# Early-stage operations moved to other places in their queues in a kernel of memory attention and a SwiGLU feed-forward layer, and two weight scans of the long units moved one beat on

## The chip, the cores and the metric

One core of one Trainium2 chip runs the program. The metric is the device time of one execution in microseconds (us). The time before is 1707.99 us, the median of three runs (1706.39, 1707.99 and 1708.14). A difference of 0.2% is 3.4 us.

## What the kernel computes

The reference takes one sequence `x` of 2048 tokens with 576 channels and makes a mix of two layers, each token with a gate of its own:

```python
g = _sigmoid((x * gate_w).sum(-1, keepdims=True))
a = _A_ref(x, A_wq, A_wk, A_wv, A_wo, A_beta)   # 32 heads of 18, four segments of 512 tokens
b = _B_ref(x, B_w_gate, B_w_up, B_w_down)       # (silu(x @ w_gate) * (x @ w_up)) @ w_down
return g * a + (1 - g) * b
```

`_A_ref` is attention inside a segment, mixed (by a learned `sigmoid(beta)` for each head) with a read of a memory matrix that sums `phi(k) v` over the segments before; `_B_ref` has 4608 hidden channels.

## The kernel before

**Numbers.** The big products work on float32 values that are split in two float16 parts, a high one (the rounded value) and a low one (the rest); a product is three float16 products (high·high, high·low, low·high) in one PSUM bank. Both parts carry a scale, a power of two, and to find it the kernel must first scan the raw weights: ACT squares a block and adds up each row (the helper at L140 for gate and up weights, L1125 in `d_look` for the down weights), PE sums across the partitions (L158), DVE and POOL make the scale of it (L150 to L154, L1137 to L1140).

**Stage 1** (0 to about 229 us) makes Q, K and V of the four segments. A segment has nine chains `n = 0..8` (Q and K) and then eight V steps (L806 on), each followed in segments 1 to 3 by `mem_step`, which reads the memory. Beside the last segment's steps lies what the next stage needs first: the operands of `x` for the first feed-forward units (`first_sum` on POOL, `first_split` with ACT L136 and DVE L137), and the split of the first unit's weights. That split is `w_make`: POOL makes sums of raw blocks (L369), ACT the high part (L373), DVE the low part (L377), SP stores both to a scratch in DRAM (L381, `wc`), for they are wanted again in the second half. `start = w_make(0)` (L799) is a list of such steps with a due number each, in rising order, and the V steps take from its front.

**Stage 2** is the feed-forward layer. It runs over two halves of the tokens and in each over 36 blocks `f` of 128 hidden channels; one (half, f) is a **unit**. Its gate and up products are done by a Strassen-like scheme with seven products, `seven(...)` (PE L1437 and L1440), and behind each product or so stands a `tick()`, eight in a unit. The eight stretches are its **beats**. In the order of one unit: product 0, ACT L1531 copies it; product 1, L1536; product 2, DVE L1540; product 3, ACT L1543; product 4, ACT L1547 and DVE L1548; ACT L1550 makes Silu, product 5, ACT L1552 Silu again; then, in units of the first half with `f % 3 == 0`, L1430 (`exp_table`) reads one number through Exp so that the table for the attention's exponentials is there; two ticks, product 6, DVE L1559 and L1560, the split of the hidden values (ACT L1305, DVE L1308).

Every third unit (`f % 3 == 0`, from f = 3) is a **long unit**. Its beats also hold 16 groups of the down projection for the three blocks before (PE L1171, DVE L1178 for the first three blocks or L1180 later) and steps of the attention (PE L895 and L1011, ACT L1015, POOL L1023 and L1115, DVE L913). PE, ACT and DVE each work through their queue strictly in the order in which the code lists it.

**What sets the order.** Work for a later beat is put in a queue with `defer(k, fn)`, to run `k` beats on. A unit has a plan, a list of `(o, fn)` that is put in with `defer(o + 1, fn)`. In the plan are the next unit's `w_make`; `r_block` (DMA of `rr` at L350, POOL sums L341 to L344, ACT L351, two stores `rc` at L348, DVE L333, a third store), which prepares a remainder of the weights; and `glance(i, k)`, k = 0..7 (L1411 to L1419): the load of a block of 128 x 640 raw weights (DMA L1416, 320 KB) into one of four buffers, and later its squares (ACT L140), which the scale of a coming group of four blocks needs. The offsets of the loads may be negative, then they lie in the unit before the long unit (L1474, `7 + o`). For the down weights, `d_load` (DMA L317, three buffers `draw`) and `d_look` are called from `tick` directly (L1502 to L1508).

**DMA.** All loads and stores are issued by SP (SyncE), one after the other. Where one has to wait (for a buffer, or for a tile to be stored), all behind it wait as well.

Of the kernel before, what the change touches and what calls it, by code (L numbers as in the profile page):

```python
# [36 lines left out]
CH = 3  # L37
# [32 lines left out]
def gated_mix(ctx, tc, xT, xrest, wf, wfr, wfh, wd, wv, wo, beta, cmask, ident, bmask, out):  # L70
# [323 lines left out]
    with ExitStack() as st:  # L394
# [326 lines left out]
        def scan_load(t):  # L721
# [3 lines left out]
            if t in (21, 30):  # L725
# [4 lines left out]
        FSPLIT = {2: [(0, 0)], 3: [(5, 0), (0, 1)], 4: [(1, 0), (4, 0)], 5: [(5, 1), (2, 0)], 6: [(1, 1), (3, 0)],  # L730
                  7: [(3, 1), (4, 1)]}
        for s in range(NSEG):
# [51 lines left out]
            if s == 3:  # L784
# [14 lines left out]
                start = w_make(0)  # L799
            for n in range(8):  # L800
# [23 lines left out]
                else:  # L824
                    if n == 4:
                        wraw_of[1] = [w_load(1, u) for u in range(2)]
                    if n == 0:
                        first_split(2, 1)
                    if n == 1:
                        first_sum(6, 1)  # L830
                    if 2 <= n < 4:
                        first_split(6, n - 2)
                    for k, t, v in ((0, rhs[0][96:], 0.0), (1, kst[0], -1.0), (3, kst[1], -1.0), (4, rhs[1][96:], 0.0)):
# [4 lines left out]
                    if n > 2:  # L838
                        for z in stack_loads(0)[2 * n - 6:2 * n - 4]:
                            nc.sync.dma_start(*z)  # L840
                    for _ in range((0, 1, 2, 2, 2, 2, 2, 2)[n]):
                        if start[0][0] < 8:
                            start.pop(0)[1]()
        flush()
        while start[0][0] < 8:
            start.pop(0)[1]()


    with ExitStack() as st:
# [560 lines left out]
        def glance(i, k):  # L1410
            f, u = 4 * i + k // 2, k % 2  # L1411
            box = []

            def load():
                box.append(x_slot(*next(looks), F32).rearrange("p a b -> p (a b)")[:, :NT * P])
                nc.sync.dma_start(box[0].rearrange("p (k n) -> p k n", n=P), wf[f][:, u])  # L1416

            return [((-2, -1, 0, 1, 3, 4, 4, 5)[k], load),
                    ((2, 2, 3, 4, 5, 6, 6, 7)[k], lambda: square(box[0], 20 + 9 * i + k))]  # L1419

# [22 lines left out]
        for o, fn in start:  # L1443
            defer(o - 7, fn)
        for pos, (half, f) in enumerate(seq):
# [49 lines left out]
            def tick():  # L1495
# [5 lines left out]
                if half == 0:  # L1501
                    g = {(0, 0): f + 2, (2, 2): f + 1, (2, 4): f + 2}.get((q, k), FT) if f > 1 else k if f == 0 and k < CH else FT  # L1502
                    if g < FT:
                        draw[g] = d_load(g)
                    if (f == 1 and 4 <= k < 4 + CH) or (f > 2 and q == 0 and 2 <= k < 2 + CH):
                        d_look(k - 4 if f == 1 else f + k - 2)
                    if (f, k) == (2, 1) or (f > 2 and (q, k) == (0, 5)):
                        d_scale(f // CH)  # L1508
# [175 lines left out]
```

## Time and profile before

| | |
|---|---|
| median of three runs | 1707.99 us |
| the profiled execution itself | 1707.77 us |
| its span | 1705.7 us |
| granted TensorE clock | 1.00 |
| start of the first units of stage 2 (f = 0, 1, 2, 3) | 229.8, 243.9, 253, 267 us |
| starts of the long units f = 6, 9, 12, 15, 18, 21 | 322, 379, 436, 493, 550, 607 us |
| size of a load of `glance`, of `raw`, of `rr` | 320, 256, 128 KB |

The span is what the trace covers, from the first instruction to the last; the execution is 2.1 us longer. A row of the timeline gives the start in us from the start of the span, the duration, engine, line, operation, output and inputs, and in brackets how long the engine had been idle before it and what released it. Rows of PE overlap: a matmul of 512 columns has a row of 0.38 us, and the next one starts 0.22 us after it. So where PE waits, the idle time in brackets is about 0.16 us less than what was lost. Rows of SP are the issue of a DMA; when it lands is seen at the engine that waits for it.

### The profile page before, as it was taken

Reading aid. Unit: us, or ns where it says so; the run is one execution under the profiler, and the core shown is the slowest. Engines: PE = TensorE matmul, PEld = TensorE weight load, DVE = VectorE, ACT = ScalarE, POOL = GpSimd, SP = SyncE. Lnnn points to the kernel's source line nnn. Section 1 sums busy time; section 2 is a strip of 40 time slices with the busy share of each in tenths; the row PEclk is TensorE's granted clock in tenths of the full one; section 3 lists DMA queues with packets and bytes.
Section 4 is the critical chain, followed back from the end, with each engine's and each line's share of the span. In section 5 each row is a group of like instructions: output and inputs, shape, how many; then the busy total and the mean of one; then the engine's idle time right before and its main releaser. Section 6 shows DMA issues by size and latency. Waiting matters only on the chain.

```text
span 1705.7 us, 35389 instructions
## 1 busy us (share of the span) xinstructions
PE 1674.5 (98%) x12269; PEld 1076.9 (63%) x12269; DVE 1300.5 (76%) x3155; ACT 1137.9 (67%) x2064; POOL 879.6 (52%) x1191
## 2 busy tenths in 40 slices
PE   9999999999999999999999999999999999999999
PEld 7898865556655665565556656656656656655587
DVE  7687666789888988898887776777767677665466
ACT  7666566777777777767775776776767676676411
POOL 3336552266656665665453655465546565554121
PEclk9999999999999999999999999999999999999999
DMA  8666776666776675446545386786597588574544
GB/s 288 225 225 226 231 244 213 219 197 182 224 229 208 171 238 193 156 121 197 170 132 178 100 197 161 158 217 157 129 213 179 123 209 182 130 165 123 156 158 146
DMA packets 349542, 314.25 MB, mean 184 GB/s; under 512 B 201268, under 2 KB 266548, under 8 KB 349364
## 3 DMA queue, kind: packets, MB, share of 16 engines
q1 hardware_dynamic: 349364, 312.00, 63.5%
q8 instruction: 96, 1.57, 0.4%
q14 instruction: 82, 0.67, 0.1%
HBM read 186.15 MB, written 99.55 MB: 167 GB/s over the span
## 4 chain that ended last, share of the span: by engine, by line
PE 76%; ACT 7%; DVE 7%; DMA 4%; issue 3%; POOL 1%; SPq 1%; DVEq 0%; ACTq 0%; POOLq 0%
PE bank L1437 30%; PE bank L1171 19%; PE bank L223 10%; PE bank L1440 5%; PE bank L895 3%; PE bank L1011 2%; PE bank L1039 1%; ACT L1550 1%; PE bank L505 1%; DMA raw<-in_wf_dram 1%; PE bank L1041 1%; ACT row L1550 1%; PE bank L973 1%; DVE ya L1180 1%; DVE junk L913 1%
## 5 line engine op out<-in xcount | busy, mean ns | idle before, releaser
L1171 PE MATMUL bank<-dw,hh 128*128 128x320 f16 (+1 forms) x2304 | 435.1, 285 | 9.5 <-DVE ya L1180 6.3
L1171 PE MATMUL bank<-dw,hl 128*128 128x320 f16 (+1 forms) x1152 | 329.0, 286 | 1.2 <-DVE hl L1308 0.6
L1115 POOL TENSOR_TENSOR p<-pe,p 128x512 f16<-128x512 f32 x220 | 272.0, 1237 | 61.7 <-DVE p L1111 34.9
L1171 PEld LDWEIGHTS <-hh 128*128 128x128 f16 x2304 | 224.8, 98 | 95.0 <-issue 15.4
L1015 ACT ACTIVATE pe<-bank 128x512 f32<-128x512 f32 x220 | 130.2, 592 | 161.8 <-PE bank L1011 149.2
L1180 DVE SCALAR_TENSOR_TENSOR ya<-bank,sc,ya 128x320 f32<-128x320 f32 x352 | 177.5, 512 | 76.3 <-PE bank L1171 74.5
L1440 PE MATMUL bank<-xr,rh 128*128 128x512 f16 x504 | 191.0, 379 | 0.0
L913 DVE CUSTOM_DVE_ANT_0 junk<-bank,cm 128x128 bf16<-128x128 f32 (+2 forms) x352 | 169.5, 481 | 20.4 <-PE bank L895 8.7
L1023 POOL TENSOR_SCALAR_AFFINE_SELECT pe<-pe 128x256 f32<-128x256 f32 (+1 forms) x220 | 88.2, 401 | 163.6 <-ACT pe L1015 156.0
L1308 DVE SCALAR_TENSOR_TENSOR hl<-hh,row 128x512 f16<-128x512 f16 x144 | 126.8, 882 | 43.6 <-ACT hh L1305 42.6
L1171 PEld LDWEIGHTS <-hl 128*128 128x128 f16 x1152 | 112.3, 97 | 30.2 <-DVE hl L1308 1.3
L895 PE MATMUL bank<-kst,qst 108*128 108x512 bf16 (+3 forms) x512 | 124.5, 299 | 5.8 <-ACT pe L1015 4.8
L1011 PE MATMUL bank<-qst,kst 111*128 111x512 bf16 (+3 forms) x352 | 103.2, 300 | 1.1 <-DVE acc L984 1.1
L369 POOL TENSOR_TENSOR ws<-raw 128x256 f32<-128x256 f32 x72 | 65.7, 913 | 64.3 <-DMA raw<-in_wf_dram 43.8
L1548 DVE TENSOR_TENSOR row<-bank,row 128x512 f32<-128x512 f32 x72 | 49.7, 690 | 63.8 <-ACT bank L1547 63.7
L223 PE MATMUL bank<-xo,qhi 128*128 128x512 f32 x288 | 92.3, 401 | 0.5 <-DVE xo L133 0.4
L1305 ACT ACTIVATE hh<-row 128x512 f16<-128x512 f32 x144 | 89.1, 619 | 1.8 <-DVE row L1560 1.7
L466 POOL TENSOR_TENSOR q<-qr,q 128x512 bf16<-128x512 f32 x36 | 47.4, 1315 | 82.9 <-ACT q L465 69.7
L1543 ACT ACTIVATE row<-bank 128x512 f32<-128x512 f32 x72 | 42.9, 596 | 68.0 <-PE bank L1440 68.0
L1440 PEld LDWEIGHTS <-rh 128*128 128x128 f16 x504 | 49.3, 98 | 59.5
L1559 DVE SCALAR_TENSOR_TENSOR row<-bank,sc,row 128x512 f32<-128x512 f32 x72 | 53.9, 749 | 43.2 <-PE bank L1440 22.2
L1547 ACT ACTIVATE bank<-bank 128x512 f32<-128x512 f32 x72 | 41.9, 581 | 64.0 <-PE bank L1440 62.0
(1104 smaller groups left out, 4265.0 us busy)
## 6 DMA issues: line engine op xcount, KB each, us to landing
xo<-in_wf_dram SPq DMA_DIRECT2D x65, 320.0 KB
raw<-in_wf_dram SPq DMA_DIRECT2D x72, 256.0 KB
dc<-dw SPq DMA_DIRECT2D x36, 432.0 KB
dw<-dc SPq DMA_DIRECT2D x36, 432.0 KB
rh<-rc SPq DMA_DIRECT2D x72, 168.0 KB
draw<-in_wd_dram SPq DMA_DIRECT2D x36, 288.0 KB
xo<-in_xT_dram SPq DMA_DIRECT2D x33, 256.0 KB
vd<-vps SPq DMA_DIRECT2D x8, 912.0 KB
```

Of the source, the lines that this page charges most:

```text
L223: nc.tensor.matmul(t, st[n], mv[n], start=(n == 0), stop=(n == 13))
L895: nc.tensor.matmul(t[:, c:c + w], qs[:KR, pr, P * i:P * i + P], ks[:KR, pr, 0:w], start=True, stop=True)
L913: nc.vector.tensor_tensor_reduce(junk.bitcast(BF)[:, :w], t[:, c:c + w], cm[:, L - w:L], 1.0, -3.0e38, OP.add, OP.max, m[:, k:k + 1])
L1011: nc.tensor.matmul(t[:, c:c + w], ks[:KR + 3, pr, P * j:P * j + P], qs[:KR + 3, pr, P * j:L], start=True, stop=True)
L1015: nc.scalar.activation(pe, t, AF.Exp, scale=SCALE)
L1115: nc.gpsimd.tensor_sub(p2, pe, p1)
L1171: nc.tensor.matmul(t, p, d[:, q, cs], start=(f == CH * c and n == 0), stop=(f == CH * c + CH - 1 and n == 2))
L1180: nc.vector.scalar_tensor_tensor(ya[:, i, cs], t, inv[c], ya[:, i, cs], op0=OP.mult, op1=OP.add)
L1305: nc.scalar.activation(hi, src, AF.Copy, scale=1.0 / STEP)
L1308: nc.vector.scalar_tensor_tensor(lo, hi, -STEP, src, op0=OP.mult, op1=OP.add)
L1437: nc.tensor.matmul(t, w[:, p, z], x[z][:, q], start=first and n == 0, stop=False, skip_group_check=True)
L1440: nc.tensor.matmul(t, rem[:, RPOS[j]], XR[j], start=False, stop=True, skip_group_check=True)
```

## The change

It moves steps; nothing is computed that was not before, and nothing is left out.

1. In the last segment of stage 1, the split of operand (4, 1) goes from Q/K chain 7 to behind V step 0; (2, 1) from behind V step 0 to 1; the sum (6, 1) from behind V step 1 to 2.
2. Of the first unit's weight split, the steps due at 7 (a store of `wc`, and one high part on ACT) leave the V steps and run in the first beat of the first unit.
3. In unit f = 1 the three `d_look` go from ticks 4 to 6 to ticks 1 to 3; in unit f = 2 `d_scale` from tick 1 to tick 0.
4. In `glance`, the loads of k = 0..3 are issued two beats earlier, and the squares of k = 4 and k = 6 come one beat later. This holds for the seven long units f = 3 to f = 21.

```diff
--- before.py
+++ after.py
@@ -728,7 +728,7 @@
         blocks = {3: [(0, 0)], 4: [(0, 1)], 5: [(0, 2), (1, 0)], 6: [(1, 1)], 7: [(1, 2)]}
         FSUM = {3: [(1, 0), (4, 0)], 4: [(2, 0), (1, 1)], 6: [(4, 1), (2, 1)], 7: [(6, 0)]}
         FSPLIT = {2: [(0, 0)], 3: [(5, 0), (0, 1)], 4: [(1, 0), (4, 0)], 5: [(5, 1), (2, 0)], 6: [(1, 1), (3, 0)],
-                  7: [(3, 1), (4, 1)]}
+                  7: [(3, 1)]}
         for s in range(NSEG):
             upd = upd_gen(s - 1) if s else None
             casts = []
@@ -824,12 +824,10 @@
                 else:
                     if n == 4:
                         wraw_of[1] = [w_load(1, u) for u in range(2)]
-                    if n == 0:
-                        first_split(2, 1)
-                    if n == 1:
+                    if n < 4:
+                        first_split(*((4, 1), (2, 1), (6, 0), (6, 1))[n])
+                    if n == 2:
                         first_sum(6, 1)
-                    if 2 <= n < 4:
-                        first_split(6, n - 2)
                     for k, t, v in ((0, rhs[0][96:], 0.0), (1, kst[0], -1.0), (3, kst[1], -1.0), (4, rhs[1][96:], 0.0)):
                         if n == k:
                             nc.gpsimd.memset(t, v)
@@ -838,11 +836,11 @@
                     if n > 2:
                         for z in stack_loads(0)[2 * n - 6:2 * n - 4]:
                             nc.sync.dma_start(*z)
-                    for _ in range((0, 1, 2, 2, 2, 2, 2, 2)[n]):
-                        if start[0][0] < 8:
+                    for _ in range((0, 1, 2, 2, 2, 2, 0, 0)[n]):
+                        if start[0][0] < 7:
                             start.pop(0)[1]()
         flush()
-        while start[0][0] < 8:
+        while start[0][0] < 7:
             start.pop(0)[1]()
 
 
@@ -1415,8 +1413,8 @@
                 box.append(x_slot(*next(looks), F32).rearrange("p a b -> p (a b)")[:, :NT * P])
                 nc.sync.dma_start(box[0].rearrange("p (k n) -> p k n", n=P), wf[f][:, u])
 
-            return [((-2, -1, 0, 1, 3, 4, 4, 5)[k], load),
-                    ((2, 2, 3, 4, 5, 6, 6, 7)[k], lambda: square(box[0], 20 + 9 * i + k))]
+            return [((-4, -3, -2, -1, 3, 4, 4, 5)[k], load),
+                    ((2, 2, 3, 4, 6, 6, 7, 7)[k], lambda: square(box[0], 20 + 9 * i + k))]
 
         looks = cycle([(6, 0), (6, 1), (5, 0), (5, 1)])
 
@@ -1441,7 +1439,7 @@
 
         draw = {}
         for o, fn in start:
-            defer(o - 7, fn)
+            defer(max(1, o - 7), fn)
         for pos, (half, f) in enumerate(seq):
             if f == 0:
                 yas[half] = yp.tile([P, 8, D], F32, name="ya")
@@ -1502,9 +1500,9 @@
                     g = {(0, 0): f + 2, (2, 2): f + 1, (2, 4): f + 2}.get((q, k), FT) if f > 1 else k if f == 0 and k < CH else FT
                     if g < FT:
                         draw[g] = d_load(g)
-                    if (f == 1 and 4 <= k < 4 + CH) or (f > 2 and q == 0 and 2 <= k < 2 + CH):
-                        d_look(k - 4 if f == 1 else f + k - 2)
-                    if (f, k) == (2, 1) or (f > 2 and (q, k) == (0, 5)):
+                    if (f == 1 and 1 <= k <= CH) or (f > 2 and q == 0 and 2 <= k < 2 + CH):
+                        d_look(k - 1 if f == 1 else f + k - 2)
+                    if (f, k) == (2, 0) or (f > 2 and (q, k) == (0, 5)):
                         d_scale(f // CH)
                     if (f, k) == (2, 7) or (f > 2 and (q, k) == (1, 3)):
                         d_back(f // CH)
```

Behind L830 the changed file's line numbers are two lower than those of before (L1416 becomes L1414, and so on). The numbers behind names are the program's own for a buffer's use and differ between the files.

What SP issues around the border from unit f = 5 to the long unit f = 6; `xo` are the loads of `glance`, `wc` the stores of split weights, `raw`, `draw` and `rr` loads of weights. Before:

```order
L381 DMA wc<-wo__3636 128x512
L312 DMA raw<-in_wf_dram 128x512
L1416 DMA xo_3715<-in_wf_dram 128x640
L381 DMA wc<-wo__3684 128x1024
L1416 DMA xo_3721<-in_wf_dram 128x640
L381 DMA wc<-wo__3699 128x1024
L317 DMA draw<-in_wd_dram 128x576
L350 DMA rr<-in_wfh_dram 128x256
L1416 DMA xo_3768<-in_wf_dram 128x640
L1155 DMA dc<-dw 128x1728
L355 DMA rh_2442<-rc 96x896
L1416 DMA xo_3786<-in_wf_dram 128x640
```

With the change:

```order
L1414 DMA xo_3686<-in_wf_dram 128x640
L317 DMA draw<-in_wd_dram 128x576
L381 DMA wc<-wo__3636 128x512
L1414 DMA xo_3703<-in_wf_dram 128x640
L312 DMA raw<-in_wf_dram 128x512
L1414 DMA xo_3719<-in_wf_dram 128x640
L381 DMA wc<-wo__3684 128x1024
L1414 DMA xo_3725<-in_wf_dram 128x640
L381 DMA wc<-wo__3701 128x1024
L317 DMA draw<-in_wd_dram 128x576
L350 DMA rr<-in_wfh_dram 128x256
```

The four loads k = 0..3 stood one by one between the other transfers, from ahead of `wc<-wo__3684` to behind `rh`, and the last two of them behind `rr`. Now all four stand ahead of `rr`, and the first of them ahead of a `draw`. The same shift stands at the other long units.

What ACT does in unit f = 9 behind the Silu (L1430 is `exp_table`, L140 the squares of `glance`, L1015 the copy of the attention's logits out of a PSUM bank). Before:

```order
L1430 ACT_TABLE_LOAD
L1430 ACTIVATE bg<-idt 128x1
L140 ACTIVATE xo_4590,sc<-xo_4590 128x640
L1015 ACTIVATE pe<-bank_4813 128x512
L1015 ACTIVATE pe<-bank_4839 128x512
L140 ACTIVATE xo_4687,sc<-xo_4687 128x640
L140 ACTIVATE xo_4689,sc<-xo_4689 128x640
L1015 ACTIVATE pe<-bank_4923 128x512
L1015 ACTIVATE pe<-bank_4958 128x512
L373 ACTIVATE wo__4981<-ws,sc 128x512
L351 ACTIVATE rt<-rr,sc 128x448
L140 ACTIVATE xo_4785,sc<-xo_4785 128x640
```

With the change:

```order
L1428 ACT_TABLE_LOAD
L1428 ACTIVATE bg<-idt 128x1
L1013 ACTIVATE pe<-bank_4812 128x512
L1013 ACTIVATE pe<-bank_4838 128x512
L140 ACTIVATE xo_4590,sc<-xo_4590 128x640
L140 ACTIVATE xo_4687,sc<-xo_4687 128x640
L1013 ACTIVATE pe<-bank_4922 128x512
L1013 ACTIVATE pe<-bank_4957 128x512
L373 ACTIVATE wo__4980<-ws,sc 128x512
L351 ACTIVATE rt<-rr,sc 128x448
L140 ACTIVATE xo_4689,sc<-xo_4689 128x640
L140 ACTIVATE xo_4784,sc<-xo_4784 128x640
```

Between `exp_table` and the first L1015 (now L1013) stood one block of squares; it is now behind the second one. One of the two blocks that followed is now behind L351, where two stand in a row.

What ACT does in unit f = 1 and at the start of f = 2; L1125 is `d_look`, L1531 the copy of a unit's first product, L1550 and L1552 Silu. Before:

```order
L1547 ACTIVATE bank_2951<-bank_2886 128x512
L1125 ACTIVATE junk,sc<-draw 128x576
L373 ACTIVATE wo__2956<-ws,sc 128x512
L1550 ACTIVATE row<-row,sc 128x512
L1552 ACTIVATE row<-bank_2924,sc 128x512
L1125 ACTIVATE junk,sc<-draw 128x576 x2
L373 ACTIVATE wo__2987<-ws,sc 128x512
L1531 ACTIVATE bank_2993<-bank_2991 128x512
```

With the change, from the second product of f = 1 on (the first `d_look` stands in the row before these):

```order
L373 ACTIVATE wo__2913<-raw,sc 128x256
L1303 ACTIVATE hh<-row 128x512
L1123 ACTIVATE junk,sc<-draw 128x576
L1541 ACTIVATE row<-bank_2888 128x512
L1123 ACTIVATE junk,sc<-draw 128x576
L373 ACTIVATE wo__2945<-raw,sc 128x512
L1545 ACTIVATE bank_2954<-bank_2886 128x512
L373 ACTIVATE wo__2958<-ws,sc 128x512
L1548 ACTIVATE row<-row,sc 128x512
L1550 ACTIVATE row<-bank_2925,sc 128x512
L373 ACTIVATE wo__2987<-ws,sc 128x512
L1529 ACTIVATE bank_2993<-bank_2991 128x512
```

The three `d_look` stood around the Silu and ahead of the next unit's first copy (L1531); now they stand in the first half of the unit, and only one high part (L373) is left between Silu and that copy.

## The prediction

> **What bounds the kernel now.** I read the page's first part, then PE's waits over the whole span, then the timeline around the places that the change touches.
>
> ```profile
> PE 1674.5 (98%) x12269; PEld 1076.9 (63%) x12269; DVE 1300.5 (76%) x3155; ACT 1137.9 (67%) x2064; POOL 879.6 (52%) x1191
> ...
> PE bank L1171 <- DVE ya L1180: 6.3, 12, 1.0
> PE bank L895 <- ACT pe L1015: 4.8, 11, 1.0
> ```
>
> PE is the bound: busy for 98% of the span, and its work is not changed. So a step that is moved can bring only what PE waits. The rows of waits give who is waited for, us in total, times and the longest; all of them are short. The change can gain a few us at most, each of them at a place that can be named:
>
> ```profile
> 216.54 1.73 PE L223 MATMUL bank<-vw,xo 128*128 128x288 f32 x11 [0.84 <-DVE r L486]
> ...
> 234.81 1.46 PE L1437 MATMUL bank<-xo,wo__2592 128*128 128x512 f16 x6 [2.02 <-ACT bank L1531]
> ...
> 255.03 1.45 PE L1437 MATMUL bank<-xo,wo__2956 128*128 128x512 f16 x6 [0.42 <-ACT row L1552]
> ...
> 257.59 0.59 PE L1437 MATMUL bank<-xo,wo__2956 128*128 128x512 f16 x2 [0.71 <-ACT bank L1531]
> ...
> 282.95 0.43 PE L1171 MATMUL bank<-dw,hh 128*128 128x320 f16 x2 [1.59 <-DVE ya L1178]
> ...
> 337.23 0.43 PE L1171 MATMUL bank<-dw,hh 128*128 128x320 f16 x2 [0.96 <-DVE ya L1180]
> ```
>
> The brackets are what PE stood idle. Add about 0.16 us to each for the overlap of the matmul before (its row of 0.38 us, 0.22 us to the next start), so the 1.59 is a loss of 1.75.
>
> **A and B: the border of the stages.** The first two waits end on DVE and ACT.
>
> ```profile
> 213.38 0.75 DVE L137 SCALAR_TENSOR_TENSOR xo<-xo,sc,xo 128x512 f16<-128x512 f32 x1
> ...
> 231.92 0.70 ACT L373 ACTIVATE wo__2711<-ws,sc 128x512 f16<-128x512 f32 x1
> 232.53 0.39 ACT L484 ACTIVATE vf<-bank 128x288 f32<-128x288 f32 x1
> ...
> 234.17 0.59 ACT L1531 ACTIVATE bank<-bank 128x512 f32<-128x512 f32 x1
> ```
>
> The L137 that leaves Q/K chain 7 stands on DVE ahead of what L486 waits for; a step of this kind holds its engine for 0.67 us, its 0.75 less the overlap. PE's wait at 216.54 is longer than that, so 0.67 goes. At the border L373 of the moved weights holds ACT for 0.61 us (231.92 to 232.53) ahead of the copies of the last V step, and behind those stands L1531, for which PE waits 2.02. Both together would be −1.28; but the last V step also follows PE and DVE, so not all of the 0.61 comes through. Bounds −0.67 and −1.28; I take −0.9, nearer to the row that stands on the chain alone. The moved L137 of (4, 1) and the others behind the V steps lie beside DVE's waits there.
>
> Most of it is given back at 255.03, since that wait doesn't begin on an engine:
>
> ```profile
> 240.38 1.28 SPq L317 DMA_DIRECT2D draw<-in_wd_dram  x3
> ...
> 251.18 0.72 POOL L369 TENSOR_TENSOR ws<-raw 128x256 f32<-128x256 f32 x1 [7.27 <-DMA raw<-in_wf_dram]
> ...
> 253.07 0.72 ACT L373 ACTIVATE wo__2956<-ws,sc 128x512 f16<-128x512 f32 x1 [1.64 <-POOL ws L369]
> ```
>
> POOL waits 7.27 us for `raw`, ACT's L373 for POOL, Silu (L1550, L1552) stands behind L373, PE behind Silu. `raw` is behind the three `draw`, which SP issues only at 240.38, when the store `vd` of the last V steps has landed. V steps that end 0.9 earlier let SP start 0.9 earlier, but the store `wc` of 256 KB that was issued before that point now goes between the `draw` (0.76 us at the 345 GB/s quoted under F). So about 0.2 stays: **A and B −0.25**, from 0 (`raw` not earlier) to −0.9.
>
> **C: the three `d_look` of unit 1.**
>
> ```profile
> 254.88 0.67 ACT L1125 ACTIVATE junk<-draw 128x576 f16<-128x576 f32 x1
> ...
> 255.67 0.68 ACT L1125 ACTIVATE junk<-draw 128x576 f16<-128x576 f32 x1
> ...
> 256.97 0.57 ACT L1531 ACTIVATE bank<-bank 128x512 f32<-128x512 f32 x1
> ```
>
> Two of them stand between Silu and L1531; one holds ACT for 0.79 us with its sum (254.88 to 255.67), both for some 1.5. PE's loss at 257.59 is 0.71 + 0.16, so without them it ends whole, and the two small matmuls of `d_scale` (some 0.1 us in PE's order) fall into the wait at 255.03. **C: −1.0** (0 if something else holds L1531, no more than the loss and those 0.1). In their new place ACT waits for PE between its steps, and the `draw` tiles were issued 5 us before.
>
> **D: the loads of f = 3.**
>
> ```profile
> 280.40 0.74 ACT L140 ACTIVATE xo<-xo 128x640 f32<-128x640 f32 x1 [0.75 <-DMA xo<-in_wf_dram]
> ...
> 281.13 0.58 ACT L1547 ACTIVATE bank<-bank 128x512 f32<-128x512 f32 x1
> ...
> 282.35 0.54 DVE L1178 TENSOR_SCALAR ya<-bank,sc 128x320 f32<-128x320 f32 x1
> ```
>
> The squares of k = 2 wait for their load, and behind them stand L1547, DVE's L1548 and L1178, for which PE waits 1.59. With all four loads issued in one go behind SP's wait, k = 2 goes ahead of two stores `dc` and of a `draw`, 432 and 288 KB, 3 us of transfers. Then L140 waits no longer, and the loss of 1.75 goes: **D −1.75** (0 if the loads still come late).
>
> **E: the squares behind Silu.**
>
> ```profile
> 398.76 1.28 ACT L1430 ACT_TABLE_LOAD   x1
> ...
> 400.17 0.72 ACT L140 ACTIVATE xo<-xo 128x640 f32<-128x640 f32 x1
> ...
> 400.89 0.58 ACT L1015 ACTIVATE pe<-bank 128x512 f32<-128x512 f32 x1
> ```
>
> PE's waits in 320 to 640 us, and in f = 9 a load of the attention's keys and the matmul that reads them:
>
> ```profile
> PE bank L895 <- ACT pe L1015: 2.3, 6, 0.4
> ...
> PE bank L895 <- DMA kst<-stk: 0.4, 1, 0.4
> ```
>
> ```profile
> 404.40 0.74 SPq L1077 DMA_DIRECT2D kst<-stk  x1
> ...
> 407.02 0.38 PE L895 MATMUL bank<-kst,qst 108*128 108x512 bf16 x1
> ```
>
> ACT reaches L1015 after the table load and one block of squares, which holds it for 0.72 (400.17 to 400.89); PE waits 0.40 for it, a loss of 0.56, in each of the six long units f = 6 to 21. Taking the squares out is more than enough. But PE then comes 0.56 earlier to the keys. In f = 15 it waits for them already (the 0.4 in the second row), so nothing is left there; in f = 9 it reads them 2.6 us after their issue, and I count half, 0.25. Four units bring 0.5 to 0.56: **E −2.4** (0 to −3.3). The second block in the later beat stands where ACT waits for PE's matmuls.
>
> **F: what the early loads push back.** In f = 6 the DMA and what follows `rr`:
>
> ```profile
> 317.00:331.00 14.00, 14.00 (x79) 7.54 (x77) 10.79 (x28) 11.96 (x25) 8.25 (x14) 1.00 1.01 345
> ```
>
> ```profile
> 321.68 0.38 SPq L381 DMA_DIRECT2D wc<-wo__3699  x1
> ...
> 324.37 0.47 SPq L350 DMA_DIRECT2D rr<-in_wfh_dram  x1
> ...
> 329.97 0.33 POOL L341 TENSOR_TENSOR rr<-rr 128x64 f32<-128x64 f32 x1 [5.21 <-DMA rr<-in_wfh_dram]
> ...
> 331.75 0.67 ACT L351 ACTIVATE rt<-rr,sc 128x448 f16<-128x448 f32 x1
> ...
> 336.03 0.68 DVE L333 SCALAR_TENSOR_TENSOR rt<-rr,sc,rt 128x448 f16<-128x448 f32 x1 [0.78 <-DMA rc<-rt]
> ```
>
> The last two numbers of the windows' row are the DMA's busy share, 1.01, and 345 GB/s. The queue is full: `rr`, 128 KB, takes 5.6 us from its issue to POOL. Two more loads of 320 KB now stand ahead of it: 655 KB at 345 GB/s are 1.9 us. POOL's four sums run to 331.7, L351 follows at once, and its two stores must land before DVE's L333 (4.28 us after L351), which stands ahead of the L1180 that PE waits for at 337.23. So f = 6 pays 1.9 less the 0.05 of slack: 1.85. In f = 15 and f = 21:
>
> ```profile
> 500.82 0.47 POOL L344 TENSOR_TENSOR rr<-rr 128x64 f32<-128x64 f32 x1
> ...
> 501.82 0.66 ACT L351 ACTIVATE rt<-rr,sc 128x448 f16<-128x448 f32 x1
> ...
> 506.84 0.69 DVE L333 SCALAR_TENSOR_TENSOR rt<-rr,sc,rt 128x448 f16<-128x448 f32 x1 [0.23 <-DMA rc<-rt]
> ```
>
> ```profile
> 614.50 0.32 POOL L344 TENSOR_TENSOR rr<-rr 128x64 f32<-128x64 f32 x1
> ...
> 616.55 0.66 ACT L351 ACTIVATE rt<-rr,sc 128x448 f16<-128x448 f32 x1
> ```
>
> In f = 15 the sums end at 501.29; 1.9 later is 503.19, and 4.28 more gives 507.47 for L333, 0.63 late. In f = 21, the tightest of the others, L351 starts 1.73 after the sums end and L333 has some slack of its own, so 1.9 costs nothing; f = 9, 12 and 18 read alike. **F +2.5**, from 0 (the delay is hidden) to +6 (3 us of delay).
>
> The Trainium skill, DMA: Bandwidth & Descriptors, section Queues, rings and completion order, says that SP has one ring on each of 16 DMA engines and that descriptors are taken in ring order. That speaks against the change: in a full queue an early issue is only an exchange of places. By its limit of some 358 GB/s from HBM (Specifications) the same 655 KB would be 1.8 us, an estimate, and the sum about 0.2 us lower; the 5.6 us of `rr` agree with the order.
>
> **The sum.** −0.25 − 1.0 − 1.75 − 2.4 + 2.5 = −2.9 us. The profiled execution (1707.77, span 1705.7) lies 0.2 below the median of 1707.99, so its stalls may stand for it: 1707.99 − 2.9 = **1705.1 us**.
>
> **The rivals.**
> 1. *Gains without the cost*: `rr` is not held back, since the loads issued earlier are also done earlier, out of the way. For it: SP has room for earlier issues, with one `draw` between the row of 321.68 (quoted under F) and `rr` at 324.37. Against: the busy share of 1.01 leaves no room on the DMA itself. −5.4, 1702.6 us.
> 2. *The gains come and are waited away*, at the next transfer: `raw` in f = 2, the loads of keys in the long units, as POOL's 7.27 and the 0.4 for `kst` show is possible, or the moved steps don't do what they say because another step holds the same wait (L1125 and L373 stand in the same queue). Only a half of C, D and E is gained, F stays: −0.25 − 2.6 + 2.5, about 1707.6 us.
> 3. *Slower*: in the full queue each block takes twice its share, 2 us and not 0.95, so `rr` is 4 us late. Then f = 6 pays 3.95, f = 15 2.7, and the slack of f = 21, 12 and 9 (about 2.2 to 2.5 with L333's own) is passed by 1.5 to 1.8 each: about +11.5 in all, net +6, 1714 us. It decides from a delay of some 2.75 us on (2.7 in f = 6, 1.5 in f = 15, 1.2 in the three others: 5.4, all that is gained). Against it: the row of 345 GB/s, in which 655 KB are 1.9.
>
> **How the numbers follow.** A measurement of this kernel can tell a change of about 0.2%, 3.4 us, from none; 1704.6 is the border. Forecast 0.41, with 1703.3 to 1706.8 as its own range, so about a third of it (0.14) counts as faster; rival 1 0.25, all faster; rival 2 0.22, all within; rival 3 0.12, slower. Faster 0.39, same 0.49, slower 0.12. The range runs from 1701.5 (rival 1 with E at its −3.3) to 1709 (rival 2 with F at +4), and leaves out rival 3 and a little at each end.
>
> **What would show it.** C: PE's row at 257.6 has no bracket, and L1531 no L1125 ahead. D: no wait for `xo` at 280 and none for L1178 at 283. E: PE's wait for L1015 gone in six units, with a wait for `kst` in f = 9 and 15. F: POOL's L341 in f = 6 near 332 on the old clock, PE's wait for L1180 behind it 2.8 and not 0.96. I am wrong if that wait stays below 1.5 (rival 1), if new waits for a DMA stand where old ones went (rival 2), or if L351 in f = 9 and 12 begins late (rival 3).

## The result: 0.25% faster, and where it came from

The changed kernel takes 1705.14 us (median of 16 runs, 1703.11 to 1708.12) and the kernel before, in 16 runs beside it, 1709.55 us (1706.39 to 1713.72). The ratio is 0.9975, with a 95% interval from 0.9967 to 0.9982: 4.3 us less, 3.1 to 5.6. The forecast was 1705.1 us, and −2.9 us against before. The first number hides something: with more runs the kernel before is at 1709.55 and not at 1707.99, so the gain was larger by 1.4 us than forecast. That 1705.1 is so close to the median is luck: the sum came out by errors that cancel.

The profiled execution has a span of 1703.6 us, against 1705.7. The page's first part, two rows of PE's waits of before, and the rows of the changed kernel that answer to those of before (line numbers two lower):

```profile
PE 1675.5 (98%) x12269; PEld 1076.7 (63%) x12269; DVE 1301.4 (76%) x3155; ACT 1137.3 (67%) x2064; POOL 878.4 (52%) x1191
```

```profile
PE bank L1437 <- ACT bank L1531: 2.9, 3, 2.0
PE bank L1171 <- DVE ya L1178: 2.6, 2, 1.6
```

```profile
PE bank L1169 <- DVE ya L1178: 6.6, 15, 0.8
...
PE bank L893 <- DMA kst<-stk: 3.7, 5, 1.3
...
PE bank L893 <- ACT pe L1013: 2.4, 5, 1.0
...
PE bank L1435 <- ACT bank L1529: 1.3, 2, 1.2
...
PE bank L1169 <- DVE ya L1176: 0.5, 1, 0.5
```

PE works as long as before (1675.5 us). The wait for the down groups of f = 3 (L1176, before 2.6 with the longest at 1.6) is 0.5, the wait for the first copy of a unit (L1529) is 1.3 and not 2.9; half of the waits for L1013 are gone. One row is new near the top: 3.7 us, in five pieces, for `kst<-stk`, the load of the attention's keys.

The same places on PE's timeline:

```profile
217.00 1.86 PE L223 MATMUL bank<-vw,xo 128*128 128x288 f32 x12 [0.38 <-DVE r L486]
...
234.39 1.46 PE L1435 MATMUL bank<-xo,wo__2592 128*128 128x512 f16 x6 [1.15 <-ACT bank L1529]
...
254.97 1.46 PE L1435 MATMUL bank<-xo,wo__2958 128*128 128x512 f16 x6 [0.65 <-ACT row L1550]
...
292.75 0.38 PE L893 MATMUL bank<-kst,qst 108*128 108x512 bf16 x1 [1.20 <-DMA kst<-stk]
...
335.60 0.43 PE L1169 MATMUL bank<-dw,hh 128*128 128x320 f16 x2 [0.61 <-DVE ya L1178]
...
405.86 0.38 PE L893 MATMUL bank<-kst,qst 108*128 108x512 bf16 x1 [1.27 <-DMA kst<-stk]
...
519.75 0.38 PE L893 MATMUL bank<-kst,qst 108*128 108x512 bf16 x1 [0.52 <-DMA kst<-stk]
```

At the border PE idles 1.15 us and not 2.02. At 257.6 and 283, where it waited 0.71 and 1.59, there is no wait left. Instead PE waits for the keys; the three longest of these waits are the rows in f = 3, 9 and 15.

To add it up without being misled by where an execution starts, I compared when PE starts the same matmul, from mark to mark, in two profiles of each kernel (the first one and a second one from the runs below, b1_before and a5_after). Negative is gained:

| stretch (times of before) | forecast | mean of two against two |
|---|---|---|
| A: the waits at 216.5 and 234.8 | −0.9 | −0.74 − 0.87 = −1.6 |
| rest of B, and C: 255.0 and 257.6 | +0.65 − 1.0 | −0.5 |
| D: f = 3 to 284.5, and the rest of f = 3 | −1.75, 0 | −2.0, +1.0 |
| E: L1015's waits in six units, given back behind them | −3.3, +0.9 | −2.5, +1.8 |
| F: `rr` in f = 6 and f = 15 | +2.5 | +0.2, +0.25 |
| sum | −2.9 | −3.35 |

In E the −2.5 is net of small waits in the six stretches; the waits for L1013 are gone in all six. The sum of −3.35 lies in the interval of the timed runs; what is left to −4.3 is spoken of below.

### The profile page after: what moved, and what is told of

The parts are those of the page before. It is cut to its first block, busy times and chain, and to the rows that moved or that the text cites. A ratio compares the mean times of both kernels' runs of the same rounds, so it can differ in the third digit from the quotient of the medians.

```text
span 1703.6 us, 35375 instructions
## 1 busy us (share of the span) xinstructions
PE 1675.5 (98%) x12269; PEld 1076.7 (63%) x12269; DVE 1301.4 (76%) x3155; ACT 1137.3 (67%) x2064; POOL 878.4 (52%) x1191
## 4 chain that ended last, share of the span: by engine, by line
PE 77%; DVE 7%; ACT 6%; DMA 5%; issue 2%; SPq 1%; POOL 1%; DVEq 0%; ACTq 0%; POOLq 0%
PE bank L1435 32%; PE bank L1169 19%; PE bank L223 10%; PE bank L1438 5%; PE bank L893 3%; PE bank L1009 2%; PE bank L1037 1%; DVE ya L1178 1%; PE bank L505 1%; DMA v<-vd 1%; PE bank L971 1%; ACT L1548 1%; DVE junk L911 1%; PE bank L1039 1%; DMA kst<-stk 1%
## 5 line engine op out<-in xcount | busy, mean ns | idle before, releaser
L1013 ACT ACTIVATE pe<-bank 128x512 f32<-128x512 f32 x220 | 130.1, 591 | 161.2 <-PE bank L1009 148.8
L1178 DVE SCALAR_TENSOR_TENSOR ya<-bank,sc,ya 128x320 f32<-128x320 f32 x352 | 177.6, 512 | 74.5 <-PE bank L1169 72.6
```

The source lines that it names most:

```text
L1013: nc.scalar.activation(pe, t, AF.Exp, scale=SCALE)
L1178: nc.vector.scalar_tensor_tensor(ya[:, i, cs], t, inv[c], ya[:, i, cs], op0=OP.mult, op1=OP.add)
```

## The experiments

Each ran on a chip beside the kernel before. Ratios are against before, with 95% intervals; 0.001 is 1.7 us. Those without a ratio (b1_before, t1_idle, a1_rrlate) are single executions, read for their traces. The first four put one part of the change alone on the kernel before.

**The squares alone.**

```diff
-                    ((2, 2, 3, 4, 5, 6, 6, 7)[k], lambda: square(box[0], 20 + 9 * i + k))]
+                    ((2, 2, 3, 4, 6, 6, 7, 7)[k], lambda: square(box[0], 20 + 9 * i + k))]
```

> Only the squares of k = 4 and k = 6 one beat later, the rest as before. If each part acts in its own place: PE's wait for L1015 goes in the six long units f = 6 to 21 (a loss of 0.5 to 0.56 each, 3.3 us in all), and in f = 9 PE waits up to 1.3 us for the load of the keys, as with the whole change: net about -2 us. If that wait for the keys comes from the early loads (another order on the DMA) and not from PE's earlier arrival: no such wait here, net -3.3 us.

Ratio 0.9987 (0.9979 to 0.9996), −2.2 us. On PE's rows 0.49 to 0.56 us go at each of the six places, and 1.1 us comes back in f = 9 ahead of the keys (0.35 comes there in the second profile of before too, which changes nothing). So the squares act in their own place, and so does the wait behind them. The forecast for E was −2.4.

**The early loads alone.**

```diff
-            return [((-2, -1, 0, 1, 3, 4, 4, 5)[k], load),
+            return [((-4, -3, -2, -1, 3, 4, 4, 5)[k], load),
```

> Only the four loads of glance two beats earlier. If the early loads only bring work forward: in f = 3 the loss of 1.75 before the first group of the down projection goes, then 1.2 to 1.4 of it comes back as a wait for the load of the keys near 293, and f = 6 stays as it was (0 for rr, against the 1.85 that I predicted): net -0.5 us. If the wait for the keys comes only with the other parts (PE some 1.1 us earlier at f = 3): net -1.7. If rr is held back by 1.9 us when nothing else moves: +1.9 at f = 6, net between 0 and +1.5.

Ratio 1.0000 (0.9989 to 1.0012). In the profile the 1.75 us at 283 go, as in the change, and all of it comes back some 12 us later:

```profile
295.24 0.38 PE L895 MATMUL bank<-kst,qst 108*128 108x512 bf16 x1 [2.13 <-DMA kst<-stk]
```

PE waits 2.13 us for the keys, and the matmuls behind are slow: the granted clock is 0.50 from 295.8 to 299.2. Together 4.0 us are lost in this execution, twice what was gained. In f = 6 it costs 0.1 us, not 1.9. Of my three cases the first holds (a gain that is given back), with a price above what I gave it.

**The three `d_look` and `d_scale` alone.**

```diff
-                    if (f == 1 and 4 <= k < 4 + CH) or (f > 2 and q == 0 and 2 <= k < 2 + CH):
-                        d_look(k - 4 if f == 1 else f + k - 2)
-                    if (f, k) == (2, 1) or (f > 2 and (q, k) == (0, 5)):
+                    if (f == 1 and 1 <= k <= CH) or (f > 2 and q == 0 and 2 <= k < 2 + CH):
+                        d_look(k - 1 if f == 1 else f + k - 2)
+                    if (f, k) == (2, 0) or (f > 2 and (q, k) == (0, 5)):
```

> Only the three d_look and d_scale earlier in f = 1 and 2. By the prediction's term C: PE's loss of 0.93 at 257.6 goes, with 0.1 for the two small matmuls: -1.0 to -1.06 up to f = 3. Rival: the transfers of f = 2 and 3 don't move with it, so PE waits as much longer at 282.95: net 0 behind f = 3.

On PE's rows −1.05 us at 257.6, as C had it, and nothing of it comes back up to f = 4 (−0.26 at 280.2 and +0.21 at 283 stand in the second profile of before as well). The time doesn't show it (ratio 1.0003, 0.9992 to 1.0014; −1 us lies inside). The profile had a surprise at the border, which this kernel doesn't touch. PE's row there and the windows from 236 to 240 us (the third number from the end is the granted clock):

```profile
236.15 2.67 PE L1437 MATMUL bank<-xo,wo__2592 128*128 128x512 f16 x6 [2.02 <-ACT bank L1531]
```

```profile
236.00:237.00 1.00, 0.85 (x3) 0.34 (x3) 0.95 (x2) 1.00 (x3) 0.94 (x2) 0.62 0.70 228
237.00:238.00 1.00, 1.00 (x4) 0.37 (x3) 0.00 (x0) 0.01 (x1) 0.92 (x2) 0.50 0.55 190
238.00:239.00 1.00, 1.00 (x3) 0.30 (x2) 0.00 (x0) 0.00 (x0) 0.92 (x3) 0.50 0.59 211
239.00:240.00 1.00, 1.00 (x5) 0.40 (x4) 0.64 (x2) 0.00 (x0) 0.59 (x1) 0.67 1.03 430
```

The wait is the 2.02 us of before, but here the clock is halved behind it, from 236.2 to 239.7, and PE loses another 1.7 us. The first profile of before has the same wait with the clock at 1.00.

**The moves at the border alone.**

```diff
-                  7: [(3, 1), (4, 1)]}
+                  7: [(3, 1)]}
...
-                    if n == 0:
-                        first_split(2, 1)
-                    if n == 1:
+                    if n < 4:
+                        first_split(*((4, 1), (2, 1), (6, 0), (6, 1))[n])
+                    if n == 2:
                         first_sum(6, 1)
-                    if 2 <= n < 4:
-                        first_split(6, n - 2)
...
-        while start[0][0] < 8:
+        while start[0][0] < 7:
...
-            defer(o - 7, fn)
+            defer(max(1, o - 7), fn)
```

> Only the moves at the border of the stages (first_split, first_sum, the steps due at 7 in the first beat). With the whole change it gave -0.57 at 216.5, -0.87 at 234.8 and +0.35 at 255.0, -1.1 in all, where I predicted -0.25 since raw would give it back. If the raw load moves with the V steps: again -1.1. If the -1.1 was the luck of one profile: -0.25.

Ratio 0.9983 (0.9973 to 0.9994), −2.9 us. On PE's rows: −0.8 up to 216.5, −0.9 at 234.8, +0.5 at 255.0, so −1.2 against the first profile of before. Then, since the loads of f = 3 are as before, PE comes earlier to the same late load:

```profile
283.51 0.43 PE L1169 MATMUL bank<-dw,hh 128*128 128x320 f16 x2 [2.73 <-DVE ya L1176]
```

ACT's square waits 1.92 us there for `xo`, and PE 2.73 and not 1.59. So by the profile nearly all is lost again by f = 4, and the timed runs say −2.9. The interval reaches to −1.0. About 0.9 us of the gap is the clock, by the estimate at the end of the account below; the rest is not settled.

**The kernel before once more**, for a second profile of one program.

> The kernel before once more, for a second profile of the same program. Where two profiles of one program differ, nothing is to be read from the change. If the differences behind f = 6 (PE's rows near 331, 337, 350 and 407 moved by 0.3 to 1.5 us also in kernels that don't touch them) are those of a single execution, this profile shows them too, with a wait for the keys in f = 9 of about 1 us; if they come from the change, it agrees with the first profile to 0.2 us there. PE's idle time of 2.02 us at the border is followed by full clock (first profile) or by some 3 us of half clock (as in the profile of the three d_look alone): either.

The places move by 0.2 to 0.6 us from execution to execution, and those that end on a DMA by up to 1: the waits at 255.0 and 257.6 are 1.1 smaller here together, and f = 9 differs by 0.35. `rr` in f = 6 shows it best (SP's issue, POOL's first sum):

```profile
324.34 0.49 SPq L350 DMA_DIRECT2D rr<-in_wfh_dram  x1
...
328.06 0.50 POOL L341 TENSOR_TENSOR rr<-rr 128x64 f32<-128x64 f32 x1 [3.33 <-DMA rr<-in_wfh_dram]
```

3.7 us from issue to use, where the first profile had 5.6. ACT gets nothing from it:

```profile
329.44 0.32 POOL L344 TENSOR_TENSOR rr<-rr 128x64 f32<-128x64 f32 x1
...
330.97 0.71 ACT L373 ACTIVATE wo__3856<-raw,sc 128x512 f16<-128x512 f32 x1
331.58 0.66 ACT L351 ACTIVATE rt<-rr,sc 128x448 f16<-128x448 f32 x1
```

POOL's sums end at 329.76, and L351 still starts at 331.58, since ACT has its own work ahead of it (L373). In the first profile the sums ended at 331.71 and L351 started at 331.75. The clock behind the border is 1.00.

**Longer waits of PE**: extra copies on ACT ahead of each unit's first copy, in the changed kernel.

```diff
             seven(a, 0)
+            for _ in range(3 + pos % 4):
+                nc.scalar.activation(junk[:, :512], XO[0][0][:, 0], AF.Copy)
             nc.scalar.activation(xx, a, AF.Copy)
```

> The changed kernel with 3, 4, 5 or 6 extra copies on ACT (in turn, from unit to unit) ahead of the copy of each unit's first product, so that PE waits there some 1 to 3.5 us in all 72 units; the output stays the same. If a wait of PE of about 2 us can halve the granted clock for about 3 us behind it, some of the waits of 1.8 to 2.4 us are followed by slow matmuls, few below 1.5 and most above 3. If the half clock behind the border was an accident of that execution: slow stretches have nothing to do with the length of the wait, and are rare (at most 2 or 3 in all).

It takes 1876.77 us, and its waits answer the question of the clock. Two of nearly the same length, and the clock behind each:

```profile
396.95 1.74 PE L1435 MATMUL bank<-xo,wo__4458 128*128 128x512 f16 x6 [2.01 <-ACT bank L1531]
...
528.70 1.45 PE L1435 MATMUL bank<-xo,wo__6176 128*128 128x512 f16 x6 [2.08 <-ACT bank L1531]
```

```profile
398.00:399.00 1.00, 1.00 (x4) 0.39 (x3) 0.03 (x1) 0.99 (x4) 0.00 (x0) 0.50 1.07 410
399.00:400.00 1.00, 1.00 (x6) 0.54 (x5) 1.00 (x2) 1.00 (x3) 0.00 (x0) 0.50 1.02 399
...
529.00:530.00 1.00, 1.00 (x7) 0.41 (x6) 0.00 (x0) 0.99 (x2) 0.00 (x0) 1.00 1.08 404
```

Behind the first the clock is 0.50 from 398.0 to 401.4, behind the second it stays at 1.00. Counted over the whole execution, a wait is followed by a slow stretch in 0 of 23 cases from 0.9 to 1.85 us, in 5 of 13 from 1.85 to 2.2, in 2 of 10 to 2.6, in 4 of 8 to 3.2 and in 6 of 8 above. A slow stretch costs 1.5 to 1.7 us where it is the only one. So the length of a wait alone does not decide.

The clock's records in the traces show what does. In each execution all changes of the clock lie on one grid with steps of 3.413 us, and the grid lies elsewhere in each execution. I added up PE's idle time in each step of t1_idle's grid, from 20 us on: 2.07 us or more ends in a fall of the clock in 14 of 14 steps, 1.91 to 2.04 us in 3 of 5, less in none. The first wait above lies whole in the step from 394.6 to 398.0; the second is cut by the end of a step at 527.7, into 1.1 and 1.0. The other runs fit: the border's wait of 2.02 us lies in one step in e3_looks (a fall) and is cut in both profiles of before (at most 1.62 in a step, no fall); 2.13 in e2_loads lies in one step (a fall), and of the 2.73 in e4_border 1.91 does (no fall). So a wait of 2 us halves the clock or not by where it falls on the grid, and behind the first 20 us a single wait below 1.9 us did so in no run.

**`rr` issued later**, in the changed kernel.

```diff
-        return [(o, lambda: nc.sync.dma_start(a[:, 0:4], wfh[h - 4])), (o + 2, sums),
+        return [(o + (o == 0), lambda: nc.sync.dma_start(a[:, 0:4], wfh[h - 4])), (o + 2, sums),
```

> The changed kernel with the first rr load of each long unit one beat later, behind a store dc (432 KB) and a load rh (168 KB). By the chain of term F (sums, L351, stores rc, L333, L1178, PE) the delay of some 1.7 us comes out at PE in f = 6 nearly whole (+1.5 or more at the row near 335.6) and with 0.5 to 1.2 in f = 15. If rr has slack in f = 6 that I overlooked: less than 0.5 there.

```profile
329.68 0.32 POOL L341 TENSOR_TENSOR rr<-rr 128x64 f32<-128x64 f32 x1 [4.62 <-DMA rr<-in_wfh_dram]
...
331.23 0.67 ACT L351 ACTIVATE rt<-rr,sc 128x448 f16<-128x448 f32 x1 [2.13 <-POOL rr L344]
...
335.49 0.69 DVE L333 SCALAR_TENSOR_TENSOR rt<-rr,sc,rt 128x448 f16<-128x448 f32 x1 [1.67 <-DMA rc<-rt]
...
336.69 0.43 PE L1169 MATMUL bank<-dw,hh 128*128 128x320 f16 x2 [3.08 <-DVE ya L1178]
```

Every link of F's chain is there: POOL waits for `rr`, ACT's L351 for POOL, DVE's L333 for the stores `rc`, PE for DVE, 3.08 us and not 0.61. PE loses 2.5 us there (2.0 if the wait of 0.5 near 331, which is gone, is taken off) and 1.6 more by the half clock behind the wait; f = 15 loses 2.05, more than the 0.5 to 1.2 that I expected. The one execution took 1713.38 us. So the chain was right: once L351 stands waiting for POOL, a delay pays in full.

**The last load of `glance` behind the loads of the keys**, in the changed kernel.

```diff
-            return [((-4, -3, -2, -1, 3, 4, 4, 5)[k], load),
-                    ((2, 2, 3, 4, 6, 6, 7, 7)[k], lambda: square(box[0], 20 + 9 * i + k))]
+            return [((-4, -3, -2, -1, 3, 4, 4, 6)[k], load),
+                    ((2, 2, 3, 4, 6, 6, 7, 8)[k], lambda: square(box[0], 20 + 9 * i + k))]
```

> The changed kernel with the last load of glance (k = 7) one beat later, so that it is issued behind the loads of the keys, and its squares one beat later. If PE waits for the keys at 292.8 and 405.9 because 320 KB stand ahead of them in the queue, these waits shrink by about 0.9 us each: net -1.5 to -2 us against the changed kernel. If they are set by the issue (SP waits for v to land, in f = 9) or by what was already in the queue: no change.

Ratio 0.9961 (0.9948 to 0.9975). SP now issues the last keys ahead of the load, and PE's waits are 0.51 and 0.54 where the changed kernel's first profile had 1.20 and 1.27; those in f = 15 and f = 18 are gone. SP's rows in f = 9, first of the changed kernel, then of this one, and PE's two waits:

```profile
400.82 0.38 SPq L1414 DMA_DIRECT2D xo<-in_wf_dram  x1
...
403.41 0.74 SPq L1075 DMA_DIRECT2D kst<-stk  x1
```

```profile
400.81 0.74 SPq L1075 DMA_DIRECT2D kst<-stk  x1
...
402.94 0.37 SPq L1414 DMA_DIRECT2D xo<-in_wf_dram  x1
```

```profile
290.85 0.38 PE L893 MATMUL bank<-kst,qst 108*128 108x512 bf16 x1 [0.51 <-DMA kst<-stk]
...
403.22 0.38 PE L893 MATMUL bank<-kst,qst 108*128 108x512 bf16 x1 [0.54 <-DMA kst<-stk]
```

PE's rows gain 0.7, 0.7, 0.7 and 0.5 us at the four places, 2.6 us against that first profile.

But in f = 9 it was not the 320 KB that the keys waited for. From issue to PE it is 2.41 us here (400.81 to 403.22) and 2.45 in the changed kernel (403.41 to 405.86). What moved is the issue: SP issues one DMA behind the other there, 0.4 to 0.8 us each, and the load's own issue stood in that row. Counted against PE's matmuls, and as the mean of two profiles of each kernel, the keys of f = 9 are issued 0.66 us earlier and PE loses 0.66 us less.

The last three ran together on one chip, to weigh this against the changed kernel.

> The changed kernel once more, on the same chip as the next two, for a second profile and a comparison beside them. If the waits for the keys (1.20 us at 292.8, 1.27 at 405.9, 0.52 at 519.8) belong to the change, they are here again, each within 0.4 us, and the time is 0.2 to 0.3% below before.

> The changed kernel with the last load of glance behind the loads of the keys, once more. If it is better by what PE no longer waits for the keys (0.7 at f = 3, 0.7 at f = 9, 0.5 and 0.5 at f = 15 and 18): 2.2 to 2.6 us below the changed kernel on this chip, 0.35 to 0.4% below before. If the first time was luck: 0.25% below before, as the changed kernel.

The changed kernel: 0.9968 (0.9955 to 0.9980), 1704.36 us. With the load behind the keys: 0.9961 (0.9948 to 0.9973), 1703.59 us. The second has the same ratio to before both times, but beside each other they differ by 0.8 us, not by the 2.2 to 2.6 expected, with intervals that overlap. So it beats before clearly, and the changed kernel only by PE's rows in f = 9. The changed kernel's second profile shows why one profile is not enough:

```profile
290.87 0.38 PE L893 MATMUL bank<-kst,qst 108*128 108x512 bf16 x1 [0.60 <-DMA kst<-stk]
...
404.58 0.38 PE L893 MATMUL bank<-kst,qst 108*128 108x512 bf16 x1 [1.44 <-DMA kst<-stk]
```

In f = 3 the wait for the keys is 0.60, half of the first time's, in f = 9 it is 1.44, and in f = 15 and f = 18 there is none, without any change. So of the four places only f = 9 is shown to gain by the move (PE loses 1.4 and 1.6 us there in the changed kernel, 0.7 and 1.0 with the load behind the keys).

**The same with `rr` issued at the head of the unit.**

```diff
-        return [(o, lambda: nc.sync.dma_start(a[:, 0:4], wfh[h - 4])), (o + 2, sums),
+        load = lambda: nc.sync.dma_start(a[:, 0:4], wfh[h - 4])
+        if o == 0:
+            load()
+        return [(o, load)] * (o > 0) + [(o + 2, sums),
```

> The same with the first rr load of a long unit issued one beat earlier, at the head of the unit. If PE's remaining wait in f = 6 (0.4 to 0.6 us for L1178) is from the early loads holding rr back (term F): it shrinks by 0.3 to 0.6 us, net -0.5 us with f = 15. If ACT reaches L351 no earlier anyway, since its own queue is full until then: no change in f = 6, net 0.

Ratio 0.9956 (0.9942 to 0.9969). PE's wait in f = 6 (line numbers three higher) is still there, and larger:

```profile
335.06 0.43 PE L1172 MATMUL bank<-dw,hh 128*128 128x320 f16 x2 [0.97 <-DVE ya L1181]
```

But the run doesn't test what it was made for. `rr` was issued at 321.68 and used at 328.01, 6.33 us later, where the second profile of the kernel above has 321.63 and 327.36. Counted against PE's matmuls it was issued 0.2 us earlier and used 0.4 later, and the wait grew with it, from 0.43 to 0.97. So whether `rr` sets what is left of that wait stays open, and this run rather speaks for it. The time is not to be told from that of the kernel above.

## Why the forecast held, step by step

Against the forecast A is 0.7 us better, B and C together 0.15 better, D 0.75 and E 1.7 worse, F 2.05 better. These errors cancel to 0.45, which is luck.

**A failed in size: the border gave more than its bound.** The step was "so not all of the 0.61 comes through … I take −0.9". It all came through, and more: −0.74 at 216.5, which is the 0.67 that I had priced, and −0.87 at 234.8, where I had allowed 0.61 and counted a little over a third of it. The sum of −1.6 lies beyond my bound of −1.28. The last V step followed ACT, and not PE or DVE: before, its L486 on DVE (at 233.32) stood waiting 0.65 us for ACT's L485, and in the changed kernel it doesn't wait. Of the 0.87, 0.61 is the L373 that leaves; the remaining 0.26 no run takes apart.

**B and C held.** The give-back at 255.0 (+0.65 forecast) and the end of the wait at 257.6 (−1.0) make −0.35; −0.5 was measured. The closeness of the two numbers is partly luck, for the same stretch is 1.1 us shorter in the second profile of before than in the first. That the wait at 257.6 goes is not luck: it loses 0.9 and 0.4 us in the two profiles of before, and nothing with the change or in e3_looks. ACT's rows of the changed kernel show one L373 between Silu and L1529, as the order had it:

```profile
254.25 0.67 ACT L1550 ACTIVATE row<-bank,sc 128x512 f32<-128x512 f32 x1
254.82 0.71 ACT L373 ACTIVATE wo__2987<-ws,sc 128x512 f16<-128x512 f32 x1
255.65 0.58 ACT L1529 ACTIVATE bank<-bank 128x512 f32<-128x512 f32 x1
```

**D held at its place and failed behind it.** The wait for L1178 at 283 is gone (−2.0 against −1.75, with 0.26 from a row at 280.2), but the step had no next wait: PE came 2 us earlier to the keys, and +1.0 is given back at 292.8. This was rival 2, which I gave only a fifth of the chance, and for half of all gains.

**E held at its place; what is given back was too small.** Behind the table load ACT now goes straight to the copy for which PE waited:

```profile
396.64 1.28 ACT L1428 ACT_TABLE_LOAD   x1
...
398.04 0.58 ACT L1013 ACTIVATE pe<-bank 128x512 f32<-128x512 f32 x1
```

The waits for it are gone in six units. I counted 0.25 us of return for f = 9 and the whole of f = 15; it was 1.4 and 1.6 in f = 9 in the two profiles, 0.5 and nothing in f = 18, which I had left out, and only 0.2 in f = 15, against the mean of the two profiles of before. The row of 2.6 us from issue to use of the keys was in my hands, and I counted half of what PE gained there as if there were slack. There was hardly any: the keys' last load is used 2.45 us after its issue when PE waits for it (403.41 on SP's rows, 405.86 on PE's).

**F failed in size: the step "655 KB at 345 GB/s are 1.9 us … f = 6 pays 1.85".** It paid 0.2, and f = 15 0.25 where I had 0.63. The chain is as I had it (the run with `rr` late); the slack in it was not, and the delay was not in full. The rows of f = 6 in the changed kernel:

```profile
322.66 0.87 SPq L350 DMA_DIRECT2D rr<-in_wfh_dram  x1
...
328.50 0.32 POOL L341 TENSOR_TENSOR rr<-rr 128x64 f32<-128x64 f32 x1 [3.23 <-DMA rr<-in_wfh_dram]
...
330.05 0.67 ACT L351 ACTIVATE rt<-rr,sc 128x448 f16<-128x448 f32 x1
...
334.40 0.69 DVE L333 SCALAR_TENSOR_TENSOR rt<-rr,sc,rt 128x448 f16<-128x448 f32 x1 [0.43 <-DMA rc<-rt]
```

From issue to POOL it is 5.84 us, against 5.60 in the first profile of before: 0.24 more, not 1.9. The other profiles tell why that pair is so close. By the semaphores in the trace, `rr` lands in f = 6 3.7, 3.9, 5.2, 5.5 and 5.5 us after its issue in the five profiles with the old order, and 5.5 to 5.8 in those with the new one; on average 4.8 and 5.65. So the 5.6 was a late one, and I added a delay to an execution that already had most of it. Against an early one the delay is there, 1.8 us, but then there is slack, which I had put at 0.05: in the second profile of before L351 starts 1.8 us behind the end of the sums, held by ACT's own L373. Counted against PE's matmuls, L351 starts within 0.2 us of the same point in all five profiles with the old order and in five with the new one, and later only in the two in which `rr` was used later still (a4_rrfirst by 0.3 us, a1_rrlate by 2). So the step that failed is "L351 follows at once": in f = 6 ACT's queue set L351, and the delayed `rr` arrives just as ACT gets there. In f = 9 it lands 3.7 and 5.4 us after its issue, 1.7 more, and slack hides that too. What makes `rr` late in some executions of the old order is open; the DMA is full ahead of its issue in either order (busy share 1.02 to 1.05 in the six us before it).

The page that I weighed, the Trainium skill, DMA: Bandwidth & Descriptors (Queues, rings and completion order), says that descriptors are taken in ring order. These runs agree: with two more loads ahead of it `rr` lands later, by 1.7 us in f = 9. It doesn't follow that the engines behind it are late by as much.

**What the sum didn't hold: the clock.** The kernel before has a wait of 2.0 us at the border in every profile, long enough to halve the clock where it lies in one step of the grid. In five profiles with the old border it happened once, at 1.7 us; the change brings the wait down to 1.15, where it happened in none. The timed runs agree. Each has its mean granted clock on record, to 0.001, which is what one slow stretch takes. It is below 1.000 in 28 of the 55 runs of the kernel before beside the experiments, and in 3 of 21 of the changed kernel; in 18 of 35 runs of the three kernels that keep the old border, and in 2 of 11 of the one that has the new border alone. So the new border is what does it. The mean clocks of 0.99935 and 0.99981 differ by some 0.8 us in a span of 1705, an estimate (0.9 for the new border alone), and bring the −3.35 to about −4.15, near the −4.3 measured. The runs at a clock of 1.000 say the same: on average 1708.4 us before and 1704.8 with the change, 3.6 apart.

The other rivals: the gains without the cost (1702.6) came nearest to how it went at f = 6, and the waits that take the old ones' place to how it went at f = 3 and 9; between them lay the forecast. The slower case, a delay of `rr` of more than 2.75 us, had its price right but for the clock: in a1_rrlate `rr` is used 2.3 us later in f = 6 and 3.2 in f = 15 than in the first profile of before, counted against PE's matmuls, which by the slack of 0.05 and 1.27 would cost 2.3 and 1.9, and PE loses 2.2 and 1.9 there. Its condition never came about with the change.

## What to carry to other kernels

A stall that is removed moves PE to its next wait, so follow the engine that was freed until the next transfer it reads, and ask how long before its use that transfer was issued; a row that shows issue and use 2.5 us apart may have no slack at all. Where a cost hangs on when a DMA lands, take two or three profiles before pricing it: one showed 5.6 us and another 3.7 for the same load. Before you price the delay of an operand, look whether the engine that uses it would have been free for it. And where SP issues without a pause, put the load that nobody is waiting for behind those that are waited for: each issue ahead of them took 0.4 to 0.8 us here.

## What the runs showed of the hardware

- A wait of PE of about 2 us can cost 1.6 us more: the granted clock falls to 0.50 for 3.41 us behind it. In these traces it falls when PE idles about 2 us (1.91 to 2.04: 3 of 5; from 2.07 on: 14 of 14) within one step of a grid of 3.413 us. The wait of 2.73 us in e4_border, cut by the grid, was not followed by it, that of 2.13 in e2_loads was. The Trainium skill, TensorE: Matmul & The Clock Gate (Part 1: The HAM clock gate), has a free-running window of about 3.4 us and a clock that falls after an idle window, and its rule is to avoid gaps of more than some 3.4 us. The grid of 3.413 us agrees with the window; but idling some 2 us of it was enough here, and the measurement decides.
- The start of an execution differs by up to 2.0 us in its first 10 us, in PE's rows, between executions whose code is the same there (up to 1.2 where the clock stays at 1.00); so spans of single profiles can't be compared to a us.
